# Chunked attention and a two-layer MLP on one core: first q and k as float32 through two other queues, the loads reordered, the first rounds written out as one list

## Chip, cores and metric

The kernel runs on one core of one Trainium2 chip. The metric is the device time of an execution in microseconds; three executions of the kernel before gave 322.51, 322.84 and 324.37 us, so the median is 322.84 us.

## What is computed

Attention runs inside chunks of 64 rows for 8 batches and 8 heads (sequence 576, head size 64), and its result, laid out as 4608 tokens of 512 features, goes through two matrix products with a leaky ReLU between them:

```
q_c, k_c, v_c = (a.reshape(8, 8, 9, 64, 64) for a in (q, k, v))
scores = (1 / sqrt(64)) * q_c @ k_c.transpose(0, 1, 2, 4, 3)
attn = exp(scores - max(scores)); attn = attn / (sum(attn) + 1e-9)
x = (attn @ v_c) as [4608, 512]          # token-major, heads side by side
h = x @ w_in                             # w_in [512, 2048]
out = maximum(0.01 * h, h) @ w_out       # w_out [2048, 512], out float32
```

All inputs lie in DRAM as float32; the kernel computes in float16 with float32 accumulation.

## The kernel before

**Units and stages.** The 4608 tokens are cut into 36 units of 128 tokens (two chunks of 64). For a unit `u` the attention is a row of short stages, each a handful of instructions. `stage_t` transposes q and k on TensorE into the PSUM tiles `qp` and `kp`, copies `qp` into the zero-padded tile `QZ` on VectorE (two copies) and `kp` into `KT` on ScalarE. `stage_s` makes the scores `Sp` (eight small matmuls), their maximum `mx` and the difference `sh` on VectorE. `stage_x` takes the exponential on ScalarE, `stage_n` the normalisation on VectorE, `stage_e` transposes the result (`tpe`, copied to `et`), and `stage_v` multiplies with v (`xp`), which ScalarE writes into `xT`, the input of the MLP.

**The MLP in chunks.** The tokens are also cut into blocks: eight of 128, two of 256, six of 512. A chunk `mm1(j, a)` makes 512 columns' worth of `h` for block `j` in one PSUM bank `hT` and evicts it through the leaky ReLU on ScalarE into `gT`. For a block of 128 tokens it is 16 matmuls and needs quarter `a` of `w_in` (columns 512a to 512a+511), so it runs as soon as that quarter is there. A chunk `mm2(j, ti, p)` adds a quarter of the second product into `oP` and needs quarter `p` of `w_out`; the last of four writes the output through SP. The list `chunks` (L186) holds their order: first `mm1` of blocks 0 to 3, then their `mm2`, then block by block. `fill(n)` takes up to `n` chunks from the head of that list, and takes none if the block at the head has tokens that no `stage_v` has made yet; it doesn't look further down the list.

**The rounds.** The loop at L285 runs 38 rounds. Round `it` holds stages of units `it`, `it - 1` and `it - 2`, with fills between them: one order for the first five rounds, another from round 5 on. Each engine executes its instructions in the order in which the program emits them.

**The loads.** All loads go through Pool's queue, since they change float32 to float16 on the way. `load_qk(u)` is one transfer for q and one for k (two each where a unit crosses a batch, as unit 4 does), `load_v(b)` two transfers of one batch, `load_w_in` two of a quarter of `w_in`, `load_w_out` one of a quarter of `w_out`. They are emitted ahead of the rounds in the order q/k 0, v 0, q/k 1, four quarters of `w_in` with q/k 2 between the second and the third, q/k 3, two quarters of `w_out`, q/k 4, the other two, q/k 5, then the zeroing of the second v tile (`zero_vb(1)` on Pool), v 1; q/k 6 to 10 follow in rounds 1 to 5. There are two v tiles: `stage_v` of units 0 to 3 needs batch 0, that of unit 4 needs batch 0 and batch 1. A transfer listed as "k_in" fills 128 partitions with eight runs of 64 values.

Of the kernel before, what the change touches and what calls it, by code (L numbers as in the profile page):

```python
# [8 lines left out]
FP16 = mybir.dt.float16  # L9
FP32 = mybir.dt.float32  # L10
ALU = mybir.AluOpType
AFT = mybir.ActivationFunctionType
# [4 lines left out]
def kernel(  # L17
# [21 lines left out]
    nc = tc.nc  # L39

    B, H, S, D = q.shape
# [3 lines left out]
    CH = 64  # L45
# [4 lines left out]
    NQZ = 3  # L50
    NVB = 2
    NIN = 9
    G = 2 * CH

    NU = n_tok // G
    BLOCKS = [128] * 8 + [256] * 2 + [512] * 6
# [10 lines left out]
    xT = sbp.tile([128, NT, n_tok], FP16, name="xT")  # L67
    qk: dict[int, tuple[bass.AP, bass.AP]] = {}

    def load_qk(u):  # L70

        both = []
        for name, src in (("q_in", q), ("k_in", k)):
            t = sbp.tile([128, H, D], FP16, name=name, tag=name, bufs=NIN)
            r0, r1 = u * G, (u + 1) * G
            cut = min(-(-r0 // S) * S, r1) if r0 % S else r1
            for a, z in ((r0, cut), (cut, r1)):
                if a < z:
                    nc.gpsimd.dma_start(  # L79
                        out=t[a - r0:z - r0],  # L80
                        in_=src[a // S, :, a % S:a % S + z - a, :].rearrange("h p d -> p h d"),
                    )
            both.append(t)
        qk[u] = tuple(both)

    def zero_vb(i, eng):
        for m in range(2):
            eng.memset(VB[i][m * CH:(m + 1) * CH, :, :, (1 - m) * CH:(2 - m) * CH], 0.0)
# [8 lines left out]
    def load_w_in(f0, f1):  # L97
        for m in range(2):
            nc.gpsimd.dma_start(  # L99
                out=w_inT[m * CH:(m + 1) * CH, :, f0:f1],  # L100
                in_=moe_w_in[m * d_model // 2:(m + 1) * d_model // 2, f0:f1].rearrange("(t d) f -> d t f", d=D),
            )

    def load_w_out(f0, f1):
        nc.gpsimd.dma_start(  # L105
            out=w_outT[:, f0:f1, :],
            in_=moe_w_out[f0 * 128:f1 * 128, :].rearrange("(fb p) m -> p fb m", p=128),
        )

    load_qk(0)  # L110
    ident = sbp.tile([128, 128], FP16, name="ident")
    make_identity(nc, ident)
    one = sbp.tile([128, 1], FP16, name="one")
    nc.vector.memset(one, 0.0)
    nc.scalar.activation(out=one, in_=one, func=AFT.Exp, bias=0.0, scale=1.0)
    zero_vb(0, nc.vector)
    for t in QZ:
        nc.vector.memset(t, 0.0)
    load_v(0)
    load_qk(1)  # L120
    load_w_in(0, 512)
    load_w_in(512, 1024)
    load_qk(2)
    load_w_in(1024, 1536)
    load_w_in(1536, 2048)
    load_qk(3)
    load_w_out(0, 4)
    load_w_out(4, 8)
    load_qk(4)
    load_w_out(8, 12)  # L130
    load_w_out(12, 16)
    load_qk(5)
    zero_vb(1, nc.gpsimd)
    load_v(1)


    gT: dict[int, bass.AP] = {}
    oP: dict[tuple[int, int], bass.AP] = {}
# [2 lines left out]
    def mm1(j, a):  # L141
        tb, r0 = BLOCKS[j], START[j]
        nf = 512 // tb
        if a == 0:
            tag, bufs, pad = ("gS", 4, 128) if tb == 128 else ("gT", 2, 512)
            gT[j] = sbp.tile([128, NFC, tb], FP16, name="gT", tag=tag, bufs=bufs, padded_shape=[128, NFC, pad])
        hT = psp.tile([128, nf, tb], FP32, name="hT", tag="mm", bufs=4)
        for i in range(nf):
            fc = nf * a + i
            for t in range(NT):  # L150
                nc.tensor.matmul(  # L151
                    out=hT[:, i, :],
                    lhsT=w_inT[:, t, fc * 128:(fc + 1) * 128],
                    rhs=xT[:, t, r0:r0 + tb],
                    start=(t == 0),
                    stop=(t == NT - 1),
                )
        nc.scalar.activation(  # L158
            out=gT[j][:, nf * a:nf * a + nf, :], in_=hT, func=AFT.Prelu, bias=0.0, scale=1.0, alpha=0.01
        )  # L160
# [19 lines left out]
    def c1(j):  # L180
        return [("mm1", j, a, 0) for a in range(NFC * BLOCKS[j] // 512)]

    def c2(j):
        return [("mm2", j, ti, p) for ti in range(BLOCKS[j] // 128) for p in range(NFC // 4)]

    chunks = c1(0) + c1(1) + c1(2) + c1(3) + c2(0) + c2(1) + c2(2) + c2(3)  # L186
    for j in range(4, len(BLOCKS)):
        chunks += c1(j) + c2(j)
    state = {"tokens": 0, "pos": 0}

# [11 lines left out]
                mm2(j, a, p)  # L202


    KT: dict[int, bass.AP] = {}
    SH: dict[int, bass.AP] = {}
    E: dict[int, bass.AP] = {}
# [3 lines left out]
    def stage_t(u):  # L211
        qt, kt = qk.pop(u)
        qp = psp.tile([128, 4, 2, CH], FP16, name="qp", tag="qp", bufs=1)
        kp = psp.tile([128, 4, 2, CH], FP16, name="kp", tag="kp", bufs=1)
        for i in range(4):
            nc.tensor.transpose(out=qp[:, i, :, :], in_=qt[:, 2 * i:2 * i + 2, :], identity=ident)  # L216
        for i in range(4):
            nc.tensor.transpose(out=kp[:, i, :, :], in_=kt[:, 2 * i:2 * i + 2, :], identity=ident)  # L218
        qz = QZ[u % NQZ]
        for s in range(2):  # L220
            nc.vector.tensor_copy(out=qz[s * CH:(s + 1) * CH, :, :, s, :], in_=qp[s * CH:(s + 1) * CH])  # L221
        KT[u] = sbp.tile([128, 4, 2, CH], FP16, name="KT", tag="KT", bufs=2)
        nc.scalar.activation(out=KT[u], in_=kp, func=AFT.Copy, bias=0.0, scale=1.0)  # L223

    def stage_s(u):
        qz, kt = QZ[u % NQZ], KT.pop(u)
        Sp = psp.tile([128, 8, CH], FP32, name="Sp", tag="Sp", bufs=1)
        for i in range(8):
            g, e, m = i // 4, i // 2 % 2, i % 2
            nc.tensor.matmul(  # L230
                out=Sp[:, i, :], lhsT=qz[:, 2 * m + g, e, :, :], rhs=kt[:, 2 * m + g, e, :], start=True, stop=True
            )
        mx = sbp.tile([128, 8], FP32, name="mx", tag="mx", bufs=2)
        nc.vector.tensor_reduce(out=mx, in_=Sp, axis=AXL.X, op=ALU.max)  # L234
        SH[u] = sbp.tile([128, 8, CH], FP32, name="sh", tag="sh", bufs=2)
        nc.vector.tensor_tensor(  # L236
            out=SH[u], in0=Sp, in1=mx.unsqueeze(2).to_broadcast((128, 8, CH)), op=ALU.subtract
        )

    def stage_x(u):  # L240
        E[u] = sbp.tile([128, 8, CH], FP16, name="ex", tag="ex", bufs=2)
        nc.scalar.activation(out=E[u], in_=SH.pop(u), func=AFT.Exp, bias=0.0, scale=SCL)  # L242
# [14 lines left out]
    def stage_e(u):  # L257
        en = E.pop(u)
        tpe = psp.tile([128, 4, 128], FP16, name="tpe", tag="ox", bufs=1)
        for i in range(4):  # L260
            nc.tensor.transpose(out=tpe[:, i, :], in_=en[:, 2 * i:2 * i + 2, :], identity=ident)  # L261
        et = sbp.tile([128, 2, 2, 2, CH], FP16, name="et", tag="et", bufs=2)
        nc.vector.tensor_copy(out=et, in_=tpe)  # L263
        ET[u] = et

    def stage_v(u):
        et = ET.pop(u)
        xp = psp.tile([128, NT, 2, CH], FP32, name="xp", tag="ox", bufs=1)
        for e in range(2):
            b, c = divmod(2 * u + e, NCH)  # L270
            for t in range(NT):
                nc.tensor.matmul(  # L272
                    out=xp[:, t, e, :],
                    lhsT=VB[b % NVB][:, t, c, :],
                    rhs=et[:, t // 2, e, t % 2, :],
                    start=True,
                    stop=True,
                )
            if c == NCH - 1 and b + NVB < B:
                load_v(b + NVB)  # L280
        nc.scalar.activation(out=xT[:, :, u * G:(u + 1) * G], in_=xp, func=AFT.Copy, bias=0.0, scale=1.0)  # L281
        state["tokens"] = (u + 1) * G


    for it in range(NU + 2):  # L285
        if it < 5:
            if it >= 2:
                stage_e(it - 2)
            if it >= 1:
                stage_s(it - 1)  # L290
            if it >= 2:
                stage_v(it - 2)
            if it >= 1:
                stage_x(it - 1)
            fill(2)
            if it >= 1:
                stage_n(it - 1)
            stage_t(it)
            if it > 2:
                fill(2)  # L300
        else:
            if it <= NU:
                stage_s(it - 1)
            fill(2)
            if it <= NU:
                stage_x(it - 1)
            stage_e(it - 2)
            if it < NU:
                stage_t(it)
            if it <= NU:  # L310
                stage_n(it - 1)
            fill(2)
            stage_v(it - 2)
            fill(2)
        if 0 < it and it + 5 < NU:
            load_qk(it + 5)
    fill(len(chunks))


# [28 lines left out]
```

## Time and profile before

| | |
|---|---|
| median of three runs | 322.84 us (322.51 to 324.37) |
| profiled execution, first to last instruction | 322.2 us; no other time of it is on record |
| TensorE matmuls (PE) | 300.4 us, 93% of the span |
| VectorE, ScalarE, Pool busy | 161.5, 165.4, 98.3 us |
| Pool's transfers (software queue) | 116416 packets, 18.36 MB |
| outputs (hardware queue) | 5184 packets, 9.44 MB |

The profile page gives busy time by engine, the span in 40 slices (each 8.05 us), the DMA queues, the chain of work that ended last, and the costliest groups of instructions. A timeline lists an engine's instructions with start and length, and behind them how long the engine sat idle and what released it. A table by windows gives busy time of each engine, the granted TensorE clock, the busy share of the DMA engines and the bytes they wrote, for each stretch of time. The DMA share can be over 1, since transfers overlap in an engine. All bytes of Pool's transfers are counted as float16, at the destination.

### The profile page before, as it was taken

To read this page: it belongs to the slowest core of one execution; us is meant where nothing else is said; L and a number is where in the kernel's file an instruction comes from. 1 tells how busy PE (TensorE), PEld (TensorE's weight loads), DVE (VectorE), ACT (ScalarE), POOL (GpSimd) and SP (SyncE) were. 2 spreads that over 40 slices of the span, in tenths; PEclk is the share of its full clock that TensorE was granted. 3 is DMA by queue.
4 is the path that set the end of the run, shared out by engine and by line. 5 is a ranking of instruction groups with operands and counts; after the bars stand their busy time and mean duration, and the time that the engine had idled before them with its cause. 6 is when DMAs were issued, how large, how long until landed. Compare 5 with 4: busy or idle time off the path is not lost.

```text
span 322.2 us, 6197 instructions
## 1 busy us (share of the span) xinstructions
PE 300.4 (93%) x2608; PEld 182.8 (57%) x2608; DVE 161.5 (50%) x330; ACT 165.4 (51%) x290; POOL 98.3 (31%) x116
## 2 busy tenths in 40 slices
PE   2477789999999999999999999999999999999995
PEld 1367685578778677555555555555554444444442
DVE  5755757666766675777667667756760000000000
ACT  2244644456665565586348734883477137316611
POOL 8763997505800560490057036000000000000000
PEclk9997979999999999999999999999999999999999
DMA  9999999955990695499169429600100020020011
GB/s 69 175 193 187 182 154 149 196 68 67 174 99 33 46 181 45 88 154 66 65 72 167 33 41 184 79 2 36 65 34 2 35 96 2 2 96 35 0 65 65
DMA packets 121627, 28.18 MB, mean 87 GB/s; under 512 B 112896, under 2 KB 116992, under 8 KB 121600
## 3 DMA queue, kind: packets, MB, share of 16 engines
q0 software_dynamic: 116416, 18.36, 77.1%
q1 hardware_dynamic: 5184, 9.44, 7.9%
q8 instruction: 20, 0.33, 0.4%
q14 instruction: 7, 0.06, 0.0%
HBM read 36.70 MB, written 9.44 MB: 143 GB/s over the span
## 4 chain that ended last, share of the span: by engine, by line
PE 86%; DMA 9%; POOL 3%; issue 1%; ACT 1%; ACTq 0%; POOLq 0%
PE oP L167 39%; PE hT L151 36%; DMA w_outT<-in_moe_w_out_dram 4%; DMA k_in<-in_k_dram 3%; DMA w_inT<-in_moe_w_in_dram 3%; PE xp L272 2%; PE Sp L230 2%; PE tpe L261 2%; PE kp L218 2%; PE qp L216 2%; POOL k_in L79 1%; POOL VB L92 1%; POOL w_inT L99 1%; POOL q_in L79 0%; POOL w_outT L105 0%
## 5 line engine op out<-in xcount | busy, mean ns | idle before, releaser
L151 PE MATMUL hT<-xT,w_inT 128*128 128x128 f16 (+2 forms) x1024 | 139.0, 293 | 4.7 <-DMA w_inT<-in_moe_w_in_dram 3.0
L167 PE MATMUL oP<-w_outT,gT 128*128 128x512 f16 x576 | 132.7, 379 | 0.0
L158 ACT ACTIVATE gT<-hT 128x512 f16<-128x512 f32 x144 | 85.8, 597 | 42.9 <-PE hT L151 42.7
L151 PEld LDWEIGHTS <-w_inT 128*128 128x128 f16 x1024 | 80.9, 102 | 44.8 <-issue 5.2
L167 PEld LDWEIGHTS <-gT 128*128 128x128 f16 x576 | 53.4, 98 | 56.7
L176 ACT ACTIVATE osb<-oP 128x512 f32<-128x512 f32 x36 | 21.5, 597 | 75.0 <-PE oP L167 69.2
L234 DVE TENSOR_REDUCE mx<-Sp 128x8 f32<-128x512 f32 x36 | 24.9, 692 | 44.5 <-PE Sp L230 44.5
L92 POOL DMA_DIRECT2D VB<-in_v_dram x16 | 18.5, 1160 | 85.9 <-PE xp L272 85.9
L79 POOL DMA_DIRECT2D k_in<-in_k_dram x40 | 35.3, 882 | 7.2 <-DMA w_inT<-in_moe_w_in_dram 2.5
L79 POOL DMA_DIRECT2D q_in<-in_q_dram x40 | 35.3, 889 | 4.7 <-DMA w_outT<-in_moe_w_out_dram 1.8
L221 DVE COPY QZ<-qp 64x512 f16<-64x512 f16 x72 | 30.1, 418 | 5.1 <-PE qp L216 4.6
L242 ACT ACTIVATE ex<-sh 128x512 f16<-128x512 f32 x36 | 22.5, 624 | 11.6 <-DVE sh L236 11.6
L281 ACT ACTIVATE xT<-xp 128x512 f16<-128x512 f32 x36 | 21.4, 593 | 11.7 <-PE xp L272 11.7
L223 ACT ACTIVATE KT<-kp 128x512 f16<-128x512 f16 x36 | 21.3, 592 | 11.6 <-PE kp L218 11.6
L247 DVE TENSOR_REDUCE z<-ex 128x8 f32<-128x512 f16 x36 | 24.7, 686 | 4.4 <-ACT ex L242 3.4
L263 DVE COPY et<-tpe 128x512 f16<-128x512 f16 x36 | 15.3, 425 | 22.4 <-PE tpe L261 22.4
L253 DVE TENSOR_TENSOR en<-ex,zi 128x512 f16<-128x512 f16 x36 | 24.9, 691 | 1.2
L236 DVE TENSOR_TENSOR sh<-Sp,mx 128x512 f32<-128x512 f32 x36 | 24.9, 691 | 1.2
L216 PE MATMUL qp<-ident,q_in 128*128 128x128 f16 x144 | 14.9, 229 | 8.7 <-DMA q_in<-in_q_dram 8.7
L230 PEld LDWEIGHTS <-QZ 128*128 128x128 f16 x288 | 13.6, 100 | 9.1 <-DVE QZ L221 1.5
L272 PEld LDWEIGHTS <-VB 128*128 128x128 f16 x288 | 13.2, 99 | 6.6 <-issue 0.4
L230 PE MATMUL Sp<-KT,QZ 128*128 128x64 f16 x288 | 14.8, 196 | 2.2 <-ACT KT L223 1.3
(22 smaller groups left out, 108.9 us busy)
## 6 DMA issues: line engine op xcount, KB each, us to landing
out_dram<-osb SPq DMA_DIRECT2D x36, 256.0 KB, 2.0
VB<-in_v_dram POOLq DMA_DIRECT2D x16, 288.0 KB, 5.7
q_in<-in_q_dram POOLq DMA_DIRECT2D x32, 128.0 KB, 6.0
k_in<-in_k_dram POOLq DMA_DIRECT2D x32, 128.0 KB, 5.9
w_inT<-in_moe_w_in_dram POOLq DMA_DIRECT2D x8, 256.0 KB, 8.5
w_outT<-in_moe_w_out_dram POOLq DMA_DIRECT2D x4, 512.0 KB, 11.1
q_in<-in_q_dram POOLq DMA_DIRECT2D x8, 64.0 KB, 6.7
k_in<-in_k_dram POOLq DMA_DIRECT2D x8, 64.0 KB, 6.2
```

Source lines behind the costliest of these rows:

```text
L79: nc.gpsimd.dma_start(out=t[a - r0:z - r0], in_=src[a // S, :, a % S:a % S + z - a, :].rearrange("h p d -> p h d"),)
L92: nc.gpsimd.dma_start(out=VB[b % NVB][m * CH:(m + 1) * CH, :, :, m * CH:(m + 1) * CH].rearrange("p h c d -> p (h c) d"), in_=v[b, m * H // ...
L151: nc.tensor.matmul(out=hT[:, i, :], lhsT=w_inT[:, t, fc * 128:(fc + 1) * 128], rhs=xT[:, t, r0:r0 + tb], start=(t == 0), stop=(t == NT - 1),)
L158: nc.scalar.activation(out=gT[j][:, nf * a:nf * a + nf, :], in_=hT, func=AFT.Prelu, bias=0.0, scale=1.0, alpha=0.01)
L167: nc.tensor.matmul(out=o, lhsT=gT[j][:, fc, ti * 128:(ti + 1) * 128], rhs=w_outT[:, fc, :], start=(fc == 0), stop=(fc == NFC - 1),)
L221: nc.vector.tensor_copy(out=qz[s * CH:(s + 1) * CH, :, :, s, :], in_=qp[s * CH:(s + 1) * CH])
L230: nc.tensor.matmul(out=Sp[:, i, :], lhsT=qz[:, 2 * m + g, e, :, :], rhs=kt[:, 2 * m + g, e, :], start=True, stop=True)
L234: nc.vector.tensor_reduce(out=mx, in_=Sp, axis=AXL.X, op=ALU.max)
L236: nc.vector.tensor_tensor(out=SH[u], in0=Sp, in1=mx.unsqueeze(2).to_broadcast((128, 8, CH)), op=ALU.subtract)
L242: nc.scalar.activation(out=E[u], in_=SH.pop(u), func=AFT.Exp, bias=0.0, scale=SCL)
L247: nc.vector.tensor_reduce(out=z, in_=ex, axis=AXL.X, op=ALU.add)
L253: nc.vector.tensor_tensor(out=E[u], in0=ex, in1=zi.unsqueeze(2).to_broadcast((128, 8, CH)), op=ALU.mult)
```

## The change

The q and k of unit 0 are no longer loaded by Pool. They are loaded as float32 into two tiles of their own, q through SP's queue and k through ACT's, and VectorE copies them into the float16 tiles. Pool begins with q/k 1. Its order becomes q/k 1, `w_in` 0, v 0, `w_in` 1, q/k 2, `w_in` 2, `w_in` 3, q/k 3, `w_out` 0, q/k 4, `w_out` 1, q/k 5, `w_out` 2, zeroing of the second v tile, v 1, `w_out` 3, q/k 6; q/k 7 to 9 come after the first rounds.

The first rounds (0 to 5) become a list, `FRONT`: a letter for a stage, a number for its unit, and `f` with the number of chunks asked of `fill`. `stage_q` is cut out of `stage_t`. The first twelve chunks follow the order in which quarters of `w_in` are loaded, across blocks 0 to 2; then come `mm1` of blocks 3 and 4, then `mm2` of blocks 0 to 4, and from block 5 on everything is as before. From round 6 on the loop is the one that was there, with q/k loaded four rounds ahead in place of five. `gT` of the small blocks has five buffers in place of four, `KT` three in place of two.

```diff
+    def rows(src, u):
+        r0, r1 = u * G, (u + 1) * G
+        cut = min(-(-r0 // S) * S, r1) if r0 % S else r1
+        return [
+            (a - r0, z - r0, src[a // S, :, a % S:a % S + z - a, :].rearrange("h p d -> p h d"))
+            for a, z in ((r0, cut), (cut, r1))
+            if a < z
+        ]
...
-    load_qk(0)
-    ident = sbp.tile([128, 128], FP16, name="ident")
-    make_identity(nc, ident)
+    first = []
+    for eng, name, src in ((nc.sync, "q_f", q), (nc.scalar, "k_f", k)):
+        t = sbp.tile([128, H, D], FP32, name=name)
+        eng.dma_start(out=t, in_=rows(src, 0)[0][2])
+        first.append(t)
     one = sbp.tile([128, 1], FP16, name="one")
     nc.vector.memset(one, 0.0)
     nc.scalar.activation(out=one, in_=one, func=AFT.Exp, bias=0.0, scale=1.0)
+    nc.vector.memset(QZ[0], 0.0)
     zero_vb(0, nc.vector)
-    for t in QZ:
-        nc.vector.memset(t, 0.0)
+    qk[0] = tuple(sbp.tile([128, H, D], FP16, name=n, tag=n, bufs=NIN) for n in ("q_in", "k_in"))
+    for t, src in zip(qk[0], first):
+        nc.vector.tensor_copy(out=t, in_=src)
+
+    load_qk(1)
+    ident = sbp.tile([128, 128], FP16, name="ident")
+    make_identity(nc, ident)
+    load_w_in(0, 512)
     load_v(0)
-    load_qk(1)
-    load_w_in(0, 512)
     load_w_in(512, 1024)
     load_qk(2)
     load_w_in(1024, 1536)
     load_w_in(1536, 2048)
     load_qk(3)
     load_w_out(0, 4)
+    load_qk(4)
     load_w_out(4, 8)
-    load_qk(4)
+    load_qk(5)
     load_w_out(8, 12)
-    load_w_out(12, 16)
-    load_qk(5)
     zero_vb(1, nc.gpsimd)
     load_v(1)
+    load_w_out(12, 16)
+    load_qk(6)
...
-        if a == 0:
-            tag, bufs, pad = ("gS", 4, 128) if tb == 128 else ("gT", 2, 512)
+        if j not in gT:
+            tag, bufs, pad = ("gS", 5, 128) if tb == 128 else ("gT", 2, 512)
...
-    chunks = c1(0) + c1(1) + c1(2) + c1(3) + c2(0) + c2(1) + c2(2) + c2(3)
-    for j in range(4, len(BLOCKS)):
+    landing = ((0, 0), (0, 1), (1, 0), (1, 1), (0, 2), (1, 2), (2, 0), (2, 1), (2, 2), (0, 3), (1, 3), (2, 3))
+    chunks = [("mm1", j, a, 0) for j, a in landing] + c1(3) + c1(4) + c2(0) + c2(1) + c2(2) + c2(3) + c2(4)
+    for j in range(5, len(BLOCKS)):
         chunks += c1(j) + c2(j)
...
+    FRONT = (
+        "t0 q0 t1 s0 x0 q1 n0 e0 s1 v0 x1 f2 n1 t2 q2 e1 s2 v1 x2 f4 n2 t3 q3 "
+        "e2 s3 v2 x3 f6 n3 t4 q4 e3 s4 v3 x4 f6 n4 t5 q5"
+    )
+    STAGES = {"t": stage_t, "q": stage_q, "s": stage_s, "x": stage_x, "n": stage_n, "e": stage_e, "v": stage_v, "f": fill}
+    for what in FRONT.split():
+        if what in ("q0", "q1"):
+            nc.vector.memset(QZ[int(what[1:]) + 1], 0.0)
+        STAGES[what[0]](int(what[1:]))
+    for u in (7, 8, 9):
+        load_qk(u)
+    for it in range(6, NU + 2):
+        if it <= NU:
+            stage_s(it - 1)
+        fill(2)
+        if it <= NU:
+            stage_x(it - 1)
+        stage_e(it - 2)
+        if it < NU:
             stage_t(it)
+            stage_q(it)
+        if it <= NU:
+            stage_n(it - 1)
+        fill(2)
+        stage_v(it - 2)
+        fill(2)
+        if it + 4 < NU:
+            load_qk(it + 4)
     fill(len(chunks))
```

More of the change, by code (lines that the diff above doesn't have):

```diff
@@ L74, in load_qk @@
             t = sbp.tile([128, H, D], FP16, name=name, tag=name, bufs=NIN)
[L75 to L82, printed above, removed]
+            for a, z, part in rows(src, u):
+                nc.gpsimd.dma_start(out=t[a:z], in_=part)
             both.append(t)
@@ L202, in fill @@
                 mm2(j, a, p)
+    P: dict[int, bass.AP] = {}
     KT: dict[int, bass.AP] = {}
@@ L218, in stage_t, with stage_q @@
             nc.tensor.transpose(out=kp[:, i, :, :], in_=kt[:, 2 * i:2 * i + 2, :], identity=ident)
-        qz = QZ[u % NQZ]
+        P[u] = qp
+        KT[u] = sbp.tile([128, 4, 2, CH], FP16, name="KT", tag="KT", bufs=3)
+        nc.scalar.activation(out=KT[u], in_=kp, func=AFT.Copy, bias=0.0, scale=1.0)
+    def stage_q(u):
+        qp, qz = P.pop(u), QZ[u % NQZ]
         for s in range(2):
             nc.vector.tensor_copy(out=qz[s * CH:(s + 1) * CH, :, :, s, :], in_=qp[s * CH:(s + 1) * CH])
-        KT[u] = sbp.tile([128, 4, 2, CH], FP16, name="KT", tag="KT", bufs=2)
-        nc.scalar.activation(out=KT[u], in_=kp, func=AFT.Copy, bias=0.0, scale=1.0)
     def stage_s(u):
@@ L282, in stage_v @@
         state["tokens"] = (u + 1) * G
[L285 to L297, printed above, removed]
-            stage_t(it)
[L299 to L316, printed above, removed]
+    FRONT = (
[17 more added lines that the diff above has]
+        if it < NU:
+            stage_t(it)
+            stage_q(it)
[6 more added lines that the diff above has]
+            load_qk(it + 4)
     fill(len(chunks))
```

## The prediction

> **What bounds the kernel now.** I read the page first: busy time by engine and the slices.
>
> ```profile
> PE 300.4 (93%) x2608; PEld 182.8 (57%) x2608; DVE 161.5 (50%) x330; ACT 165.4 (51%) x290; POOL 98.3 (31%) x116
> ...
> PE   2477789999999999999999999999999999999995
> ...
> DMA  9999999955990695499169429600100020020011
> ```
>
> TensorE (PE) is full from the seventh slice (48 us) on, and the DMA engines are full until then. The idle gaps of PE's timeline add up to 17.9 us before 48 us and to none after it; the rest is the tail of 3.8 us. So a change of the front is worth what it moves the moment from which PE never waits again. The chain of waits says what sets that moment.
>
> ```profile
> 9.55 8.21 DMA w_inT<-in_moe_w_in_dram
> ...
> 19.80 12.31 DMA w_outT<-in_moe_w_out_dram
> ...
> 32.40 8.27 DMA k_in<-in_k_dram
> ...
> 40.71 0.41 PE kp L218 x4
> ...
> 41.20 0.60 ACT KT L223
> 41.80 0.50 ACT xT L281
> ...
> 42.34 3.49 PE hT L151 x32
> ```
>
> The chain is one stream of transfers, which ends when k of unit 5 lands at 40.7. Then come 1.63 us until the next hT group (KT and xT on ScalarE first), and that group takes 3.49 us. PE's timeline shows what the same work costs at other times:
>
> ```profile
> 31.30 1.95 PE L151 MATMUL hT<-xT,w_inT 128*128 128x128 f16 x32
> ...
> 47.91 0.39 PE L216 MATMUL qp<-ident,q_in 128*128 128x128 f16 x4
> 48.13 0.39 PE L218 MATMUL kp<-ident,k_in 128*128 128x128 f16 x4
> 48.35 1.89 PE L167 MATMUL oP<-w_outT,gT 128*128 128x512 f16 x8
> ```
>
> Start to next start, two hT groups take 1.80 us at full clock (31.30 to 33.10) and 3.32 at 42.34 (to 45.66). Unit 6 is transposed at 47.91 without a wait. The table by windows (the five busy columns with counts, granted clock, DMA share, GB/s) prices the stream and that clock:
>
> ```profile
> 3.00:4.00 1.00, 0.00 (x0) 0.00 (x0) 0.85 (x2) 0.00 (x0) 0.93 (x4) 1.00 1.54 99
> ...
> 9.00:10.00 1.00, 0.00 (x0) 0.00 (x0) 0.66 (x1) 0.30 (x1) 1.00 (x3) 1.00 2.39 153
> ...
> 14.00:15.00 1.00, 0.88 (x16) 0.71 (x14) 0.58 (x2) 0.09 (x1) 0.61 (x1) 1.00 1.24 205
> ...
> 39.00:40.00 1.00, 0.68 (x13) 0.51 (x11) 0.42 (x1) 0.70 (x3) 1.00 (x2) 1.00 1.77 120
> ...
> 43.00:44.00 1.00, 1.00 (x12) 1.00 (x10) 0.21 (x1) 0.00 (x0) 1.00 (x3) 0.50 2.42 154
> ```
>
> No data moves before 3.0 us; q, k and v move at 154 GB/s, weights at 205. So q+k of a unit (262 KB) cost 1.70 us, a batch of v (590 KB) 3.83, a quarter of weights (524 KB) 2.56. Check: between k of unit 4 (33.98) and k of unit 5 (40.71) lie two quarters and one q+k, 6.82 against 6.73 measured. Between the second quarter of w_in (17.89) and k of unit 4 lie four quarters and three q+k, 15.34 against 16.09, so 0.75 is lost there. Carried on, v 1 and q+k 6 put k of unit 6 at 40.71 + 3.83 + 1.70 = 46.2, ahead of its use.
>
> **The change, part by part.** What is done when PE comes to the transposes of unit 6? In the old order t0 to t5, s0 to s5, e0 to e4, v0 to v3 and 16 hT groups. In the new one exactly the same: f2, f4, f6 take twelve, and the second f6 gets only block 3's four, because block 4 is next and needs v4. In round 6 the first two fills find block 4 still closed, so between e4 and t6 PE has nothing to do; in the old order it had oP chunks. Hence the gain is the time of t6 before against after, less what the restart costs. I need the landing of k 6, the last in the new list.
>
> *q and k 0 on SP and ACT.* Pool loses two issues (1.01 and 0.89 us), and q/k 1 take their places, so undisturbed they land where k 0 did, at 6.34. The hardware queue isn't seen with 256-byte runs. They are as many runs as Pool's q+k 0, 1.70 us of the engines at full pace; between 3 and 6 us the share is 1.5 of 2.4, which leaves room for 1.1. I take 0.6 of delay; the ends are 0 (all before 3.0 or in the gaps) and 3.4 (twice the bytes written, all ahead of Pool's). A rule speaks against this part: the Trainium skill, "DMA: Bandwidth & Descriptors", section "Issuing engines are not separate DMA queues", says that all queues share the same 16 engines and only issue time is saved. By it alone the delay would be the whole 1.70 and the forecast 1.1 us later; the room in the rows above is why I take less.
>
> The issues cost SP and ACT about 0.34 each (the output's row); the table load behind ACT's (1.28) ends near 2.4, its first use is KT near 7. The two casts on VectorE are not in the trace: 0.42 (128x512 copy, et) to 0.69 (128x512 float32, sh) each; I take 0.69. Behind the VB and QZ memsets, they run from about 5.0, and s0 comes near 7.9 against 7.63. That costs nothing: v0 waits for v 0 at 13.3 (below), and from s0 to e0 were 5.3 us.
>
> *Order of the loads.* From k 1 at 6.9: w_in 0 9.5, v 0 13.3, w_in 1 15.9, k 2 17.6, w_in 2 20.2, w_in 3 23.5 (with the 0.75), k 3 25.2, w_out 0 27.7, k 4 29.4, w_out 1 32.0, k 5 33.7, w_out 2 36.2, v 1 40.1, w_out 3 42.6, k 6 44.3. That is eight quarters, two v, five q+k: 20.5 + 7.7 + 8.5 + 0.75 = 37.4. Ends: 6.34 + 36.6 = 43.0 and 6.34 + 3.4 + 37.4 = 47.1.
>
> *Zeroing on Pool.* It takes 4.10 us (33.26 to 37.36 before) with v 1, w_out 3, q/k 6 and all later Pool loads queued behind it.
>
> ```profile
> 32.40 0.87 POOL L79 DMA_DIRECT2D k_in<-in_k_dram  x1 [1.67 <-DMA w_outT<-in_moe_w_out_dram]
> 33.26 4.10 POOL L88 MEMSET VB<- 64x2304 f16 x2
> 37.32 2.30 POOL L92 DMA_DIRECT2D VB<-in_v_dram  x2
> ```
>
> Pool waits for the transfer eight issues back (k_in here, for the w_out that landed at 32.11). So w_out 2 is issued when w_out 0 has landed, 27.7, the memsets end near 32.6, and v 1 moves from 34.4 (1.75 later, as the first q did). Landings trail the bytes by about 1.5, so w_out 2 covers until 34.7. This is as tight as before, where the 39 to 40 window fell to 120 GB/s, 0.2 us lost. Without that cover it costs the memsets' 4.1, less what is queued.
>
> *PE up to t6.* k 3 at 25.2 opens t3, e2, s3, v2 (to 26.5) and xT (about 1.0); six groups at 0.90 end at 32.9; t4, e3, s4, v3 to 34.7, xT, four groups to 39.3; t5, its copy to QZ (0.86), s5, e4 to 41. Then PE waits 3.3 us for k 6. A half-clock stretch on the way (up to 1.7) is eaten by that wait.
>
> *Restart.* As in the rows at 40.71: 1.63 us from kp to the next hT, and two groups at half clock, 3.32; together 4.95. At full clock it is 3.43. I take 4.95, since the old front lost its clock there after gaps of 0.32, 0.46 and 1.00 us only. The Trainium skill, "TensorE: Matmul & The Clock Gate", section "HAM oscillation", puts the loss behind idle gaps of over 3.4 us; by it the old stretch at 42.34 would have stayed fast, and the new time would be 1.5 us lower.
>
> *Sum.* New: 44.3 + 4.95 = 49.3 for the end of (t6, v4, two hT groups). Old: 47.91 + 0.44 + 0.23 + 1.80 = 50.4. The gain is 1.1 us of the span of 322.2; with the runs' median 0.6 above that span, 322.84 becomes 321.7. Behind this point all matmuls and tail are the same, and q/k 7 to 9 follow at 1.70 each, against rounds of over 6 us. The ends: 43.0 + 3.43 gives 318.9; 47.1 + 4.95 gives 324.5.
>
> **Rivals.** *The stream is faster, and PE sets the pace.* If small runs moved at 205, k 6 would land at 6.9 + 6.69 MB / 205 = 39.5; PE goes through t6 at 41 and ends the two groups at 41 + 0.44 + 0.23 + 1.0 + 1.8 = 44.5: 5.9 faster, 316.9. For it: earlier quarters now have work. Against: every window of q, k or v shows 154.
>
> *The hardware queue is slow with short runs.* Its packets (nearly all 2 KB) took 7.9% of 16 x 322.2 us, 78.6 ns each over 5184; Pool's 34 ns. If a 256-byte run costs 78.6 too, q and k need 128 x 78.6 = 10.1 us of every engine. Without overlap, and with 2.1 of room, the stream is 8.0 late: k 6 at 51.7, the end 6.3 later than the old one, 329.1. With the overlap of 2.4 it is 4.2 - 2.1, 323.2. It turns the result to slower from 1.7 us of delay, and past 1% from 4.9.
>
> *Nothing moves*: the stream carries the same bytes, and t6 lands where the restart eats the gain; that is the middle of the forecast's own range, not a case apart.
>
> **How the numbers follow.** About 1%, 3.2 us, is what a measurement can tell from no change. The forecast has 0.70: 0.06 of it beyond 1% faster, 0.62 within, 0.02 slower. The fast stream has 0.13, the slow queue 0.17, of which 0.04 stays within 1%. So faster 0.19, same 0.66, slower 0.15. The range takes the forecast's ends and reaches a little into both rivals: 318.2 to 325.5.
>
> **What would show it.** Right: PE idle right before qp and kp of unit 6, ended by DMA k_in near 44; hT at half clock after it; no oP before block 4's hT. q_f and k_f landed by 5, k 1 by 7. Wrong: k 6 before 41 with t6 unwaited (fast stream); k 1 after 9 (slow queue); a gap in GB/s around 33 to 36 (the memsets uncovered); or any idle time of PE after 50 us, which I put at none.

## The result, and the profile after

The changed kernel takes 327.5 us (median of four, 326.87 to 327.97) against 322.71 us: a ratio of 1.0135, 95% interval 1.0104 to 1.0166. It is slower by 4.8 us where 1.1 us faster was forecast.

The page of the profile after, busy time and slices (span 325.6 us, so a slice is 8.14 us):

```profile
PE 299.6 (92%) x2608; PEld 182.0 (56%) x2608; DVE 160.5 (49%) x332; ACT 165.8 (51%) x290; POOL 97.0 (30%) x114
...
PE   2178849999999999999999999999999999999994
...
DMA  9999999915990694499089349900100020020011
```

TensorE is busy for as long as in the profile before (299.6 against 300.4 us; a second profile, below, has 297.6). What was added is waiting: its idle gaps add up to 21.7 us where they were 17.9, and the sixth slice shows it above all (4 where it was 8). TensorE's timeline there:

```profile
43.69 0.41 PE L244 MATMUL Sp<-KT,QZ 128*128 128x64 f16 x8 [0.73 <-ACT KT L232]
43.93 0.39 PE L275 MATMUL tpe<-ident,en 128*128 128x128 f16 x4
47.40 0.61 PE L227 MATMUL qp<-ident,q_in 128*128 128x128 f16 x4 [3.09 <-DMA q_in<-in_q_dram]
48.36 0.61 PE L229 MATMUL kp<-ident,k_in 128*128 128x128 f16 x4 [0.35 <-DMA k_in<-in_k_dram]
48.76 0.64 PE L286 MATMUL xp<-et,VB 128*128 128x64 f16 x8
50.14 3.41 PE L160 MATMUL hT<-xT,w_inT 128*128 128x128 f16 x32 [0.74 <-ACT xT L295]
53.38 0.40 PE L244 MATMUL Sp<-KT,QZ 128*128 128x64 f16 x8
```

This is the picture that the prediction drew: nothing between tpe of unit 4 and the transposes of unit 6, a wait for q and k of unit 6, then two hT groups at half clock. Only the times differ, and both ends of the wait have moved: TensorE is through tpe of unit 4 at 44.3 and not at 41, k 6 lands at 48.3 and not at 44.3, and the two groups end at 53.4 and not at 49.3. The chain of waits says the same (start, length, what):

```profile
37.98 0.86 POOL q_in L84
38.84 9.47 DMA k_in<-in_k_dram
...
48.36 0.62 PE kp L229 x4
...
49.01 0.60 ACT KT L232
49.60 0.50 ACT xT L295
...
50.14 3.41 PE hT L160 x32
```

The chain runs through the same stream of transfers as before, and that stream is later than its prices. The table by windows shows several stretches below 154 GB/s; these two have the least busy DMA engines between 7 us and the landing of k 6:

```profile
7.00:8.00 1.00, 0.92 (x10) 0.95 (x11) 0.00 (x0) 0.00 (x0) 1.00 (x2) 1.00 0.96 129
...
36.00:37.00 1.00, 0.74 (x14) 0.56 (x11) 0.66 (x2) 0.90 (x2) 1.00 (x2) 1.00 0.71 109
```

The first is w_in 0, which should move at 205; the second is the end of w_out 2, behind which Pool zeroes a tile.

### The profile page after: what moved, and what is told of

It reads as the page before. It is cut to its first block, busy times and chain, and to the rows that moved or that the text cites. A ratio compares the mean times of both kernels' runs of the same rounds, so it can differ in the third digit from the quotient of the medians.

```text
span 325.6 us, 6166 instructions
## 1 busy us (share of the span) xinstructions
PE 299.6 (92%) x2608; PEld 182.0 (56%) x2608; DVE 160.5 (49%) x332; ACT 165.8 (51%) x290; POOL 97.0 (30%) x114
## 4 chain that ended last, share of the span: by engine, by line
PE 83%; DMA 9%; POOL 5%; issue 1%; ACT 1%; ACTq 0%; POOLq 0%
PE oP L176 38%; PE hT L160 35%; DMA w_inT<-in_moe_w_in_dram 3%; DMA w_outT<-in_moe_w_out_dram 3%; DMA k_in<-in_k_dram 3%; PE xp L286 2%; PE kp L229 2%; PE Sp L244 2%; PE tpe L275 2%; PE qp L227 2%; POOL VB L94 1%; POOL VB L90 1%; POOL w_inT L101 1%; POOL k_in L84 1%; POOL w_outT L107 0%
## 5 line engine op out<-in xcount | busy, mean ns | idle before, releaser
L160 PE MATMUL hT<-xT,w_inT 128*128 128x128 f16 (+2 forms) x1024 | 136.9, 291 | 3.5 <-ACT xT L295 3.5
L84 POOL DMA_DIRECT2D k_in<-in_k_dram x39 | 33.7, 863 | 6.8 <-DMA w_outT<-in_moe_w_out_dram 2.2
L84 POOL DMA_DIRECT2D q_in<-in_q_dram x39 | 34.0, 875 | 3.0 <-DMA w_inT<-in_moe_w_in_dram 1.1
L256 ACT ACTIVATE ex<-sh 128x512 f16<-128x512 f32 x36 | 22.5, 625 | 13.7 <-DVE sh L250 13.7
L275 PE MATMUL tpe<-ident,en 128*128 128x128 f16 x144 | 14.4, 224 | 4.7 <-DVE en L267 4.7
L286 PEld LDWEIGHTS <-VB 128*128 128x128 f16 x288 | 13.5, 100 | 8.8 <-issue 2.3
L244 PEld LDWEIGHTS <-QZ 128*128 128x128 f16 x288 | 13.4, 100 | 8.4 <-DVE QZ L237 2.6
```

The source lines that it names most:

```text
L84: nc.gpsimd.dma_start(out=t[a:z], in_=part)
L160: nc.tensor.matmul(out=hT[:, i, :], lhsT=w_inT[:, t, fc * 128:(fc + 1) * 128], rhs=xT[:, t, r0:r0 + tb], start=(t == 0), stop=(t == NT - 1),)
```

## The experiments

After the result there were four candidates. The hardware queues set the stream back. The order of the transfers does. The computation that runs beside them does. Or the stream is not the point at all, but TensorE's queue, in which nothing else can run in the wait.

**One part undone, one part alone.** First q and k of unit 0 back on Pool:

```diff
-    for eng, name, src in ((nc.sync, "q_f", q), (nc.scalar, "k_f", k)):
...
+    load_qk(0)
     one = sbp.tile([128, 1], FP16, name="one")
...
-    for t, src in zip(qk[0], first):
-        nc.vector.tensor_copy(out=t, in_=src)
```

> The changed kernel with q and k of unit 0 loaded by Pool again, ahead of q/k 1; all else stays. Order theory (the stream is late because of how weights and short runs follow each other, not because of the hardware queues): everything behind lands as late as in the changed kernel and 1.3 to 1.7 us more, k of unit 6 near 49.8, span near 327. Hardware-queue theory (the two float32 transfers set the 16 DMA engines apart, and a second hardware queue costs about 1.1 us outside the span): the sixteen shares of a transfer land within 1 us of each other again, k 6 near 45.5, span near 323, and the time outside the span falls from 1.75 to about 0.6 us.

It takes 328.57 us, a ratio to the kernel before of 1.0161 (1.0126 to 1.0196); k 6 lands at 49.0, and 1.74 us of the time lie outside the span. The trace has the landing of a transfer in sixteen steps, its shares: from w_in 0 to v 1 they are 2 us and more apart, though the hardware queues are gone. Then the opposite, the kernel before with only these loads changed:

> The kernel before with only this part of the change: q and k of unit 0 as float32 through SP and ACT, cast on VectorE; Pool's order and the rounds are those of before. Order theory: k of unit 5 lands about 1 us earlier than 40.66, span near 321.2, time outside the span as before. Hardware-queue theory: the shares of the first Pool transfers land up to 3 us apart, k 5 near 43, span 324 or more, and 1.1 us more outside the span.

It takes 321.36 us, ratio 0.9961 (0.9932 to 0.9989); k 5 lands at 39.45 in place of 40.66:

```profile
39.50 0.40 PE L226 MATMUL kp<-ident,k_in 128*128 128x128 f16 x4 [0.50 <-DMA k_in<-in_k_dram]
```

So the hardware queues bring the stream forward, by 1.2 us here and by 0.7 in the run above (49.0 against 48.3), and the rival that made them slow is out. In time the gain here is about 1.3 us and clear of noise; the run above is 1.1 us slower than the changed kernel, which their intervals don't tell apart. The time outside the span doesn't hang on them either.

**v ahead of w_in 0.**

```diff
+    load_v(0)
     load_w_in(0, 512)
-    load_v(0)
```

> The changed kernel with one swap in Pool's list: v of batch 0 ahead of the first quarter of w_in, as in the kernel before. Order theory: the second half of v 0 lands near 11.5 and the shares stay within 1 us; k of unit 6 near 45.5 in place of 48.3, span near 323. Hardware-queue theory: the shares are apart as before the swap, k 6 near 48, span near 325.5.

327.4 us, ratio 1.0114 (1.0073 to 1.0155), k 6 at 48.0: no difference. The order theory in this form falls; the numbers are those of its rival, but that had fallen with the two runs before.

**Work for the wait.** The chunks put back as they were, second products ahead of block 4:

```diff
-    chunks = [("mm1", j, a, 0) for j, a in landing] + c1(3) + c1(4) + c2(0) + c2(1) + c2(2) + c2(3) + c2(4)
-    for j in range(5, len(BLOCKS)):
+    chunks = [("mm1", j, a, 0) for j, a in landing] + c1(3) + c2(0) + c2(1) + c2(2) + c2(3)
+    for j in range(4, len(BLOCKS)):
```

> The changed kernel with one list changed: the second products of blocks 0 to 3 stand ahead of block 4, as in the kernel before, so that TensorE has chunks that wait for no further unit. If the empty stretch before the transposes of unit 6 is the cost: two or more oP chunks run ahead of s5 and two more ahead of t6, TensorE waits under 1.5 us for k 6 and keeps its clock, and the span falls by 3.5 (four chunks) plus 0.7 (the wait for xT of unit 4) plus up to 1.6 (clock), to 320 to 321.5. If the landing of k 6 alone sets the time, whatever TensorE does before it: 324 or more.

321.55 us, ratio 0.9944 (0.9917 to 0.9972): 5.9 us below the changed kernel, and faster than the kernel before. Its TensorE timeline:

```profile
43.46 1.89 PE L176 MATMUL oP<-w_outT,gT 128*128 128x512 f16 x8
45.19 0.39 PE L227 MATMUL qp<-ident,q_in 128*128 128x128 f16 x4
...
46.77 1.03 PE L176 MATMUL oP<-w_outT,gT 128*128 128x512 f16 x4
48.07 1.02 PE L176 MATMUL oP<-w_outT,gT 128*128 128x512 f16 x4 [0.27 <-DMA w_outT<-in_moe_w_out_dram]
...
49.99 0.40 PE L229 MATMUL kp<-ident,k_in 128*128 128x128 f16 x4 [0.45 <-DMA k_in<-in_k_dram]
50.23 1.89 PE L176 MATMUL oP<-w_outT,gT 128*128 128x512 f16 x8
```

In this run k 6 lands even later, at 49.95, and it hardly matters: four oP chunks stand in the former gap, and the clock stays full behind it (two chunks of oP in 1.89 us). A late stream costs what TensorE has no work for.

**The reference.** Every profile above of which the whole time is on record had 1.7 to 1.8 us outside the span; the prediction had reckoned with 0.6 for the kernel before. So it was profiled again:

> The kernel before, unchanged, for further profiles of it beside the others. Every profiled run since has 1.73 to 1.81 us of time outside its span, with and without the second hardware queue. If that is a constant of the launch, the runs of the kernel before show 1.7 to 1.8 as well, and its typical span is near 321.0, so the profiled execution that the prediction used (322.2) was a slow one by 1.2 us. If the hardware queues cost it, the kernel before shows near 0.6.

322.68 us; in the profiled execution the span is 320.8 and the whole 322.54, so 1.74 outside. TensorE's timeline of this execution:

```profile
40.81 0.40 PE L218 MATMUL kp<-ident,k_in 128*128 128x128 f16 x4 [0.50 <-DMA k_in<-in_k_dram]
41.04 0.40 PE L272 MATMUL xp<-et,VB 128*128 128x64 f16 x8
42.44 1.95 PE L151 MATMUL hT<-xT,w_inT 128*128 128x128 f16 x32 [1.00 <-ACT xT L281]
...
46.47 0.39 PE L216 MATMUL qp<-ident,q_in 128*128 128x128 f16 x4
```

The same instructions, nearly the same waits; but the groups at 42.4 take 1.95 us, where the first profile had 3.49. The first profile was of an execution 1.4 us longer than the usual one, by that half-clock stretch.

**The loads alone.** Now the stream without the computation. In these kernels only the transposes of units 0 to 6 are left, since a kp group starts when its k has landed; their times as a whole are not used. The first has the new list:

```diff
+    for u in range(7):
+        stage_t(u)
-    FRONT = (
...
-    fill(len(chunks))
```

> The changed kernel's loads alone: it leaves out all of the computation but the transposes of units 0 to 6 (with their copies to KT), which show when q and k land; the output is filled from k of unit 6. If the list of transfers itself makes the stream late: k of unit 6 lands at 47 to 48.5, as in the changed kernel (48.3). If what the other engines do meanwhile makes it late: 44 to 45.5, near the 44.3 of the prediction.

The second has the old one, from v 0 on:

```diff
+    load_v(0)
     load_qk(1)
...
     load_w_in(0, 512)
-    load_v(0)
     load_w_in(512, 1024)
...
     load_w_out(4, 8)
-    load_qk(5)
+    load_qk(4)
     load_w_out(8, 12)
+    load_w_out(12, 16)
+    load_qk(5)
     zero_vb(1, nc.gpsimd)
     load_v(1)
-    load_w_out(12, 16)
     load_qk(6)
```

> The same loads without the computation, with Pool's list in the order of the kernel before (q and k of unit 0 through SP and ACT): it leaves out the same parts. If the list makes the difference: k of unit 6 lands at 44.5 to 45.5, two to three us ahead of the new list's run. If the other engines' work makes it: within 0.7 us of the new list's run.

Transposes of k of units 1, 2, 5 and 6 with the new list:

```profile
7.68 0.58 PE L229 MATMUL kp<-ident,k_in 128*128 128x128 f16 x4 [0.26 <-ACT KT L232]
...
20.43 0.61 PE L229 MATMUL kp<-ident,k_in 128*128 128x128 f16 x4
...
35.68 0.61 PE L229 MATMUL kp<-ident,k_in 128*128 128x128 f16 x4 [0.23 <-DMA k_in<-in_k_dram]
...
47.81 0.61 PE L229 MATMUL kp<-ident,k_in 128*128 128x128 f16 x4 [0.35 <-DMA k_in<-in_k_dram]
```

and with the old list:

```profile
11.00 0.61 PE L229 MATMUL kp<-ident,k_in 128*128 128x128 f16 x4 [0.44 <-DMA k_in<-in_k_dram]
...
17.84 0.61 PE L229 MATMUL kp<-ident,k_in 128*128 128x128 f16 x4 [0.40 <-DMA k_in<-in_k_dram]
...
37.99 0.61 PE L229 MATMUL kp<-ident,k_in 128*128 128x128 f16 x4
43.68 0.61 PE L229 MATMUL kp<-ident,k_in 128*128 128x128 f16 x4 [0.35 <-DMA k_in<-in_k_dram]
```

The same bytes through the same queues, and k 6 lands 4.1 us apart: the list does it, not the computation. Beside the computation it does the same: the kernels of "The old list with the new rounds" and "Work for the wait" differ in the list alone, and k 6 lands at 45.4 and at 49.95. In the old list the prices hold: k 1 to k 2 (two quarters, one q+k) 6.84 against 6.82, k 5 to k 6 (one v, one q+k) 5.69 against 5.53. In the new list two stretches fail, both with the same content (two quarters, one v, one q+k; 10.65 by the prices). From k 1, which landed at 7.03 (its transposes wait for KT), to k 2 it takes 13.4, and from k 5 to k 6 12.13. Between them, k 2 to k 5 takes 15.25 against 15.34. The two losses differ. Before k 2 only the later shares lose: the first share of k 2 comes 10.4 us after the first of k 1 (10.6 in the changed kernel), as the prices have it, the last 13.4 after the last. Before k 6 the first share is as late as the last (12.4).

**The old list with the new rounds.** Pool's old order, the new list of rounds, and oP ahead of block 4:

```diff
-    chunks = [("mm1", j, a, 0) for j, a in landing] + c1(3) + c1(4) + c2(0) + c2(1) + c2(2) + c2(3) + c2(4)
+    chunks = [("mm1", j, a, 0) for j, a in landing] + c1(3) + c2(0) + c2(1) + c2(2) + c2(3)
...
+    load_v(0)
     load_qk(1)
...
     load_w_in(0, 512)
-    load_v(0)
     load_w_in(512, 1024)
```

> The changed kernel with two of its parts put back: Pool's list in the order of the kernel before (q and k of unit 0 stay on SP and ACT), and the second products of blocks 0 to 3 ahead of block 4. w_out 3 then lands near 37.7 and k of unit 6 near 45.4. If the two losses are separate (the late stream, and the empty stretch): TensorE never waits for w_out, comes to the transposes of unit 6 at 44 to 46, and the span is 318.5 to 320, 1 to 2.5 below that with the new list. If the list matters only through k of unit 6, which the oP chunks cover already: 320.5 to 321.5.

322.52 us, ratio 0.9974 (0.9954 to 0.9994), and a span of 320.7 in the profile: a miss. The number is the one of the second expectation, but not for its reason: k 6 lands at 45.4 as expected, and TensorE comes to its transposes only at 49.5, without a wait. The new list of rounds puts t1 ahead of s0, and with the old list k 1 lands late, so s0 (`Sp`) starts at 11.85 where it started at 7.63:

```profile
10.75 0.61 PE L227 MATMUL qp<-ident,q_in 128*128 128x128 f16 x4 [4.17 <-DMA q_in<-in_q_dram]
...
11.85 0.64 PE L244 MATMUL Sp<-KT,QZ 128*128 128x64 f16 x8
```

By this timeline the new rounds need the new list's early q/k 1.

**What in the list.** One swap in each list, loads alone; first q/k 2 between v 0 and w_in 1:

```diff
     load_v(0)
+    load_qk(2)
     load_w_in(512, 1024)
-    load_qk(2)
```

> The changed kernel's loads alone (it leaves out the computation but the transposes of units 0 to 6, like the two runs of loads), with q/k 2 moved between v 0 and w_in 1. With the new list the stretch from k 1 to k 2 took 12.7 us where the prices give 10.65, and k 3 landed at 27.2. Junction theory (weights directly behind a batch of v cost about 2 us, with q/k between them nothing): k 2 near 15.8, k 3 near 25.2, k 6 near 45.8. If weights directly ahead of v cost it: k 2 near 17.8, k 3 near 27.2, k 6 near 47.8.

k 2 at 18.9, k 3 at 28.1, k 6 at 49.2: worse than either expectation, and the junction theory falls. (The 12.7 us count from the transposes of k 1; from its landing they are 13.4.) Then the old list with q/k 1 and v 0 swapped:

```diff
-    load_v(0)
     load_qk(1)
+    load_v(0)
     load_w_in(0, 512)
```

> The old list's loads alone (it leaves out the same parts), with q/k 1 moved ahead of v 0, so that w_in 0 comes directly behind v 0 and no weights stand ahead of v. Junction theory: about 2 us lost, k 2 near 19.8 (old list: 17.8) and k 6 near 45.7 (43.7). If weights ahead of v cost it: k 2 and k 6 stay within 0.5 us of 17.8 and 43.7.

k 2 at 20.5, k 6 at 46.0. This is what the fallen theory expected, and one swap that costs 2.3 us. With the same two moves of q/k in the full kernel (q/k 2 ahead of w_in 1, q/k 6 ahead of w_out 3), with and without the old order of chunks:

```diff
     load_v(0)
+    load_qk(2)
     load_w_in(512, 1024)
-    load_qk(2)
...
     load_v(1)
+    load_qk(6)
     load_w_out(12, 16)
-    load_qk(6)
```

> The changed kernel with only q/k 2 put between v 0 and w_in 1 and q/k 6 between v 1 and w_out 3; the chunks keep the change's order. Junction theory: k of unit 6 lands at 41.8 to 43.5 in place of 48.3, TensorE comes to its transposes at 42 to 44 with under 1 us of wait, and the span is 318.5 to 320.5 (5 or more below the changed kernel). If only the place of q/k 6 ahead of w_out 3 counts (2.56 us) and the junctions cost nothing: k 6 near 45.7, span near 323.

> The changed kernel with q/k 2 between v 0 and w_in 1, q/k 6 between v 1 and w_out 3, and the second products of blocks 0 to 3 ahead of block 4. Junction theory: v 0 lands near 13.5, the first hT starts near 15, q and k 6 no longer hold TensorE, span 318 to 319.5, below both kernels. Otherwise: as with the chunks' order alone, 320.5 to 321.5.

The list alone gives 325.45 us, ratio 1.0076 (1.0050 to 1.0101); its profiled span, 323.7, is far from the 318.5 to 320.5 expected. k 6 lands at 43.3, and TensorE never waits for it. That landing lies in the range of the theory that the loads alone had just refuted; 2.56 of the 5.0 us gained are the quarter that no longer stands ahead of q/k 6, and the rest was not taken apart. The timeline shows why the run is still slower than the kernel before:

```profile
44.84 0.39 PE L275 MATMUL tpe<-ident,en 128*128 128x128 f16 x4
45.06 0.39 PE L227 MATMUL qp<-ident,q_in 128*128 128x128 f16 x4
45.28 0.39 PE L229 MATMUL kp<-ident,k_in 128*128 128x128 f16 x4
46.84 0.39 PE L286 MATMUL xp<-et,VB 128*128 128x64 f16 x8 [1.17 <-DVE et L277]
48.20 3.42 PE L160 MATMUL hT<-xT,w_inT 128*128 128x128 f16 x32 [0.97 <-ACT xT L295]
51.46 0.40 PE L244 MATMUL Sp<-KT,QZ 128*128 128x64 f16 x8
```

The stretch without chunks stays; TensorE now waits in it for VectorE and ScalarE, and loses its clock (3.42 us for the two groups). It reaches unit 6 only at 45.1, so by this run k 6 at the 44.3 of the prediction would not have been enough. With the chunks moved too it is 321.65 us, 0.9972 (0.9945 to 0.9999), and its profiled span 320.0, where 318 to 319.5 were expected (v 0 landed at 15.4, not 13.5): not below the chunks alone (321.55), though k 6 lands at 43.5 here and at 49.95 there. Of the variants that beat the kernel before, none is clear of the others.

Three more runs of the loads went after the cause in the list:

```diff
     load_w_in(0, 512)
+    load_qk(2)
     load_v(0)
+    load_qk(3)
     load_w_in(512, 1024)
-    load_qk(2)
     load_w_in(1024, 1536)
     load_w_in(1536, 2048)
-    load_qk(3)
```

> The changed kernel's loads alone (it leaves out the computation but the transposes of units 0 to 6), with v 0 put between q/k 2 and q/k 3, and those two ahead of w_in 1: no weights stand next to v 0 on either side. By the prices from k 1 at 7.0: k 2 at 11.3, k 3 at 16.8, k 4 at 28.8 (new list: 31.4), k 6 near 46 with the second batch left as it is. Neighbour theory (weights next to v, ahead or behind, cost about 2 us): k 3 at 16.5 to 17.3 and k 4 at 28.5 to 29.3. If another cause sets the engines apart in the first 10 us, whatever v's neighbours are: k 4 at 31 or later.

```diff
-    load_v(0)
...
-    zero_vb(1, nc.gpsimd)
-    load_v(1)
```

> The new list's loads alone without both batches of v and without the zeroing on Pool (it leaves out these too, beside the computation). By the prices from k 1 at 7.0: k 2 at 13.8, k 3 at 20.6, k 4 at 24.9, k 5 at 29.2. Neighbour theory: within 0.7 us of these. If weights and short runs in turn lose time without v as well: k 3 at 22 or later, k 5 at 31 or later.

```diff
     load_w_in(0, 512)
+    zero_vb(1, nc.gpsimd)
     load_v(0)
...
     load_w_out(8, 12)
-    zero_vb(1, nc.gpsimd)
```

> The new list's loads alone (it leaves out the same computation) with the zeroing of the second v tile moved between w_in 0 and v 0, so that Pool writes no descriptors of v while w_in 0 moves; v 0 then starts near 10.8, some 2.6 us of the stream empty. If Pool's issuing of v slows w_in 0: the sixteen shares of w_in 0 land within 1 us of each other (1.9 in the new list's run), and v 0 lands whole near 14.7. If weights beside short runs in the DMA engines are the cause: the shares of w_in 0 stay 1.5 us or more apart. Either way v 1 has no memset ahead of it, and the stretch from k 5 to k 6 falls from 12.1 us to about 11.3.

With v 0 fenced by q/k on both sides k 3 lands at 19.9 and k 4 at 31.4, as late as ever: the neighbours of v are not it. Without any v, k 2 lands at 16.8 (13.8 by the prices), k 3 at 22.7 (20.6) and k 5 at 31.2 (29.2):

```profile
7.22 0.61 PE L226 MATMUL kp<-ident,k_in 128*128 128x128 f16 x4 [0.29 <-DMA k_in<-in_k_dram]
...
16.82 0.61 PE L226 MATMUL kp<-ident,k_in 128*128 128x128 f16 x4 [0.97 <-DMA k_in<-in_k_dram]
```

That is 2 to 3 us late, so v isn't needed. It is what the last expectation of that run says of weights and short runs in turn; but they stand in turn in the old list too, without the loss. With the zeroing moved, the shares of w_in 0 stay 1.5 us apart, and v 0 lands whole at 18.2, not 14.7: Pool's issuing of v isn't it. But that run settles the second stretch. Its transposes of k of units 5 and 6:

```profile
38.27 0.61 PE L229 MATMUL kp<-ident,k_in 128*128 128x128 f16 x4 [0.23 <-DMA k_in<-in_k_dram]
...
49.02 0.61 PE L229 MATMUL kp<-ident,k_in 128*128 128x128 f16 x4 [0.35 <-DMA k_in<-in_k_dram]
```

10.75 us in place of 12.13, against 10.65 by the prices: the loss between k 5 and k 6 was the zeroing on Pool. Each is one run; two others with the zeroing in place took 11.9 (v 0 between q/k 2 and q/k 3) and 13.1 (q/k 2 behind v 0). The loss before k 2 stays open. It came with every list that had q/k 1 ahead of v 0, or no v, and with none that had v 0 ahead of q/k 1; why is not shown.

## Why the prediction was wrong, point by point

*What bounds the front*: right. The chain ends with k of unit 6; TensorE sits between tpe of unit 4 and these transposes and restarts at half clock. From kp to the end of the two groups it took 5.02 us (4.95 forecast). The half clock came after a wait of 3.1 us, and in the run with only the list changed after waits of 1.2 and 1.0, so 4.95 was the right choice over 3.43.

*PE up to t6, "to 41"*: wrong, and covered up by the late stream. TensorE was through e4 at 44.3: v 0 landed at 16.2 where 13.3 was counted, t3 began at 27.7 and not at 25.2, and from there to the end of e4 went 16.6 us, not 15.8. That it then waited 3.1 us for q 6, with 3.3 forecast, is luck, since both ends of the wait were over 3 us late. The run with only the list changed shows what this step was worth: k 6 at 43.3, TensorE there at 45.1, and still 0.8% slower than before.

*q and k on SP and ACT*: right in kind and size. They landed at 4.5 and 5.2 (forecast: by 5), k 1 at 6.9 as forecast, s0 at 7.88 (7.9). The casts took 0.43 us each, near the lower of the two rows, not the 0.69 taken. k 1 came 0.6 us after the 6.3 at which k 0 had landed. The Trainium skill's rule in "DMA: Bandwidth & Descriptors" that queues share the engines did not decide it (by it alone the prediction had 1.70): the DMA engines moved nothing before 3.0 us in the kernel before, and the part alone gains 1.3 us.

*Order of the loads, "20.5 + 7.7 + 8.5 + 0.75 = 37.4"*: this step failed. From k 1 to k 6 it was 41.4. The prices were right for each kind of transfer, and for the old list as a whole; they don't add up for the new one. In the changed kernel k 1 to k 2 took 13.7 and k 5 to k 6 12.5, each 10.65 by the prices, and the 0.75 taken over from the old stream did not come on top. The first loss, 3.1 us, has no term in the sum; in the changed kernel only the later shares have it, and its cause is open. The second is the zeroing. The range's upper end allowed for a slow hardware queue, and nothing for the list.

*Zeroing on Pool*: wrong. I found it covered with 0.3 us to spare. With the loads alone it cost 1.4 (12.13 less 10.75), in the changed kernel up to 1.9. The cover was counted to the last share of w_out 2: in the changed kernel its first share landed at 35.8 and its last at 38.4, so the DMA engines that were done early had nothing left while Pool zeroed; that reading goes by the shares, and the cost alone was tried.

*The old end of the front, "50.4"*: wrong by 1.4. It was read from an execution with a half-clock stretch which the usual one doesn't have; in the second profile the same point comes at 46.47 + 2.47 = 48.9. The 0.6 us between span and median was taken for a constant of the launch; it is 1.7 to 1.8, and the difference should have said that the profiled execution was a long one.

*The sum*: -1.1 forecast, +4.0 for the stream, +0.1 for the restart, +1.4 for the reference is 4.4; 4.8 were measured. The other 0.4 is the tail, which the prediction took to be the same: from the start of the last matmul to the end it is 4.62 us, against 4.26 in both profiles of the kernel before. All seven profiles of full kernels with q and k through SP and ACT have 4.62 to 4.66, the one variant without them 4.23; what in the tail takes longer was not looked into.

*The rivals*: neither of the two with a price came. The slow hardware queue had the right effect (a stream late by more than 1.7 us makes it slower) from the wrong cause. What turned the lateness into time was seen in the text (TensorE has nothing to do between e4 and t6) but not priced as an edit of its own: block 4 ahead of the second products. Put back, it is worth 5.9 us, more than any other part that was tried.

## What to carry to other kernels

An engine that works in order needs something ready in its queue at each point where a transfer could be late: moving work up to where its data land first can leave the next wait empty, and that decided more here than when the data came. Prices of transfers hold for the order in which they were measured; a kernel with the loads alone tells what a new order does. Before a profile serves as the reference, its span should be set against the spread of the times, and a second profile taken where they don't fit.

## What the runs showed of the hardware

- The sixteen shares of one transfer landed within 1.0 us of each other through the whole old list when it ran alone. With the new list they were 0.6 us apart at k 1, 1.9 at w_in 0 and 3.6 at v 0, and still 2.4 at k 6; a transfer counts as landed with its last share.
- In the old list with one swap, between 11.6 and 12.3 us, packets of 128 bytes took 32 ns each as always, but came one at a time, 42 to 127 ns apart and not 12 to 13 as just before, while weights moved as well; which DMA engine moved a packet the trace doesn't tell. Of the first 512 packets of w_in, 98 ns each as a rule, the longest took 604 ns there, 1136 in the new list's loads and 252 in the old list's. One of 1111 ns also stands in the second profile of the kernel before, so a slow packet alone is no sign of the loss.
- The granted clock fell to half at 42.2 us in one execution of the kernel before and not in another, after nearly the same waits (0.3, 0.5 and 1.0 us). The Trainium skill, "TensorE: Matmul & The Clock Gate", Part 1, says that the window over which activity is judged runs free of the kernel's start; the two executions agree with that. The stretches at half clock ahead of the tail lasted 3.41 us (two in that execution, one in the run with only the list changed), 6.83 (the changed kernel, and the two runs with q and k 0 back on Pool and with that part alone) or 10.24 (the run with v 0 ahead of w_in 0).
- The granted clock reads 1.00 from the start, but the first hT groups don't run at full speed: 16 matmuls took 1.87 us at 15.56 in the kernel before, and 1.05 at 22.15.
- A transfer of 256 KB in 256-byte runs on SP's or ACT's queue landed 3.7 and 4.5 us after its issue and held its issuer for 0.42 and 0.49 us.
